# Half-array matmuls for the sorted keys, and for the values of batch 1, in a fused Sinkhorn-attention and feed-forward kernel

## The chip, the cores and the metric

The kernel runs on one core of a Trainium2 chip. The core has a matrix engine (TensorE, rows PE for the matmuls and PEld for the loads of their weights), a vector engine (VectorE, DVE), a scalar engine (ScalarE, ACT), a general engine (GpSimd, POOL) and a queue engine (SyncE, SP) that issues DMAs. Each takes its instructions in order. Two memories on the core matter here: SBUF, which holds operands, and PSUM, into which the matmuls write, from which VectorE and ScalarE read, and which has eight banks of 512 float32 in each of 128 partitions. The metric is device time in microseconds for one launch.

## The reference

Inputs are q, k and v of 4 batches x 8 heads x 768 tokens x 64, one 8x8 matrix `sort_net` for each head, and the weights of a feed-forward layer (512 to 2048 to 512).

```
P = sort_net; 5 times: P = exp(P - rowmax); P /= its row sums; P /= its column sums
k_sorted[i] = sum over j of P[i, j] * k_block[j]      # 8 blocks of 96 tokens, each head
v_sorted[i] = sum over j of P[i, j] * v_block[j]
attn = softmax(q_block @ k_sorted_block.T / 8)         # within a block of 96 tokens
x = (attn @ v_sorted_block), heads side by side        # 3072 x 512
out = (s * relu(x @ w_in)**2 + b) @ w_out
```

## The kernel before

All of k of a batch lies in one SBUF tile `RAW["k", b]`: 128 partitions are (head, block, z), where z says which half of a block's 96 tokens; the free axes are 48 tokens c and 64 values d. `build_pd` makes from P a matrix `PD[b]` of 128 x (e, z, g), 2 x 2 x 32 columns: head 2a+e, half z, and g = (a, i) for the pair of heads a and the sorted block i. It is zero except where row and column belong to the same head and half, so that a matmul with `PD[b]` as the moving operand sorts the blocks of all heads at once. Row half 0 to 63 holds heads 0 to 3, that is the pairs a = 0 and 1 and the columns g = 0 to 15; row half 64 to 127 holds the others.

**Keys.** `k_piece` and `k_banks` (batch 0) are not touched. `k_pairs` (batches 1 to 3) takes 16 tokens c. For each two of them it issues one matmul (L314): weights are 128 partitions x (2 tokens x 64 values), 128 columns of `PD` move, and the result is (token parity u, d) x (e, z, g). After 8 such matmuls, which fill two banks of the tile `tpp`, four copies move it into `KS`, 64 partitions x 512 elements each: the two of e = 0 by one engine and the two of e = 1 by the other (L203 is the copy on ScalarE, L205 the one on VectorE, both inside the helper `evac`). The letters "DA" or "AD" say which engine has which.

**Values.** `v_piece` (batches 0 and 1) needs values with d outside and tokens inside. For batch 1 `permute` makes this tile `VP[1]`: 2 x 16 columns d on ScalarE (L195), the other 32 on GpSimd in four copies (L197). Then one column d at a time is the weight (128 partitions x 64), and two matmuls, one for each z, write the two halves of the PSUM partitions (L340): 32 matmuls for 16 columns d. One copy of 112 x 1024 moves them to `VS`. Batches 2 and 3 sort values by another way (`v_tiles`, `v_back`), which stays.

**The order.** The schedule is written out by hand: every engine executes its instructions in the order in which the Python code issues them. For a batch b the two feed-forward halves run as `ffn1(2b)`, `ffn1(2b+1)`, `ffn2(2b)`, `ffn2(2b+1)`. `ffn2` (L525) is three row blocks m of 16 matmuls (128 x 512, `ops`); after every fourth there is a slot, 0 to 11, in which work of the next batch is issued. After the 16th of a block, and before the work of that slot, `store` (L550) has VectorE take `ops` out of PSUM. `halves(n)` returns the slots of batch n: K pieces `KP`, V pieces `V`, score pieces `SC` (matmul L405, exp on ScalarE L413), `P` (attention times values, L450, then a reciprocal L455 and a product L456 on VectorE), `TD` (a transposing DMA of the result, L476), and `PDB`, which is `build_pd` of the batch after, seven small VectorE instructions (L275 to L294).

**Buffers.** The PSUM pool `psa` has three buffers of two banks. K, V, score and P pieces and the tiles of `ffn1` take them in turn, so that each has to wait until the one three before it has been read out. The pool `psb` has two buffers of one bank; `ops` alternates between them.

**Queries.** For batches 1 to 3 q comes through two transposing DMAs per batch (`q_dma`, L484, tile `qt`) issued on SP behind the DMAs of `v_back` (L379, L383).

Of the kernel before, what the change touches and what calls it, by code (L numbers as in the profile page):

```python
# [9 lines left out]
FP = mybir.dt.float32  # L10
# [12 lines left out]
def kernel(  # L23
# [12 lines left out]
    nc = tc.nc  # L36

    B, H, S, D = q.shape
# [9 lines left out]
    C2 = BLK // 2  # L48
    GAP = 64
    KR = GAP + C2  # L50
    NG = NHP * NB
    VW = D + 2
    CK = 16
# [15 lines left out]
    psa = ctx.enter_context(tc.tile_pool(name="psa", bufs=3, space=bass.MemoryType.PSUM))  # L69
# [14 lines left out]
    RAW = {}  # L84
# [34 lines left out]
    VP = [const.tile([128, D, GAP], BF, name=f"vp{i}") for i in range(2)]  # L119
    KS = [const.tile([128, NG, 2, GAP], BF, name=f"ks{i}") for i in range(2)]  # L120
    VS = [const.tile([KR, 2 * NG, VW], BF, name=f"vs{i}") for i in range(2)]
# [67 lines left out]
    idv = ident.rearrange("p (a e j z) -> p a e j z", a=NHP, e=2, j=NB)  # L189

    def permute(eng, b, src, cs=slice(0, C2), ds=slice(0, D)):
        o = VP[b % 2][:, ds, cs]
        i = src[:, cs, ds].rearrange("p c d -> p d c")
        if eng is nc.scalar:
            eng.copy(out=o, in_=i)  # L195
        else:
            eng.tensor_copy(out=o, in_=i)  # L197
# [3 lines left out]
    def evac(eng, out, in_):  # L201
        if eng == "A":
            nc.scalar.copy(out=out, in_=in_)  # L203
        else:
            nc.vector.tensor_copy(out=out, in_=in_)  # L205

    def q_banks(b, half, engs):
# [3 lines left out]
        for u in range(2):  # L211
# [13 lines left out]
            out=jsel, in_=ident.rearrange("p (h j z) -> p j h z", h=H, j=NB), axis=AX.XY, op=ALU.add),  # L225
        lambda: nc.vector.tensor_reduce(
            out=bm.rearrange("p (e z a) -> p e z a", e=2, z=2),
# [26 lines left out]
    PD = {}  # L254
# [54 lines left out]

    def k_pairs(b, c0, engs):  # L310
        m = CK // 2
        ps = psa.tile([128, m, 2, 2 * NG], FP, tag="a", name="tpp")
        for j in range(m):
            nc.tensor.matmul(out=ps[:, j].rearrange("p e g -> p (e g)"),  # L314
                             lhsT=RAW["k", b][:, c0 + 2 * j:c0 + 2 * j + 2, :].rearrange(
                                 "p c d -> p (c d)"),
                             rhs=PD[b].rearrange("p e z g -> p (e z g)"), start=True, stop=True)
        for e in range(2):
            for u in range(2):
                evac(engs[e],  # L320
                     KS[b % 2][e * 64:(e + 1) * 64, :, :, c0 + u:c0 + CK:2],
                     ps[u * 64:(u + 1) * 64, :, e].rearrange("p c (z g) -> p g z c", z=2))

    def k_banks(b, c0, engs):
        for u, eng in enumerate(engs):
# [10 lines left out]
    def v_piece(b, d0, eng, halves=None):  # L336
        ps = psa.tile([128, CK, 2 * NG], FP, tag="a", name="tv")
        for d in range(CK):
            for z in range(2):
                nc.tensor.matmul(out=ps[z * GAP:(z + 1) * GAP, d, :],  # L340
                                 lhsT=VP[b % 2][:, d0 + d, :], rhs=PD[b][:, :, z, :],
                                 start=True, stop=True)
        if halves is None:
            evac(eng, VS[b % 2][:, :, d0:d0 + CK], ps[0:KR].rearrange("p d g -> p g d"))
            return None

        def half(h, eng):
            hs = slice(h * HB, (h + 1) * HB)
            evac(eng, VS[b % 2].rearrange("p (g i) w -> p g i w", i=NB)[:, :, hs, d0:d0 + CK],
                 ps[0:KR].rearrange("p d (g i) -> p g i d", i=NB)[:, :, hs])  # L350

        half(0, eng)
        return lambda eng: half(1, eng)

    NC = C2 // 8

# [34 lines left out]
    def s_piece(b, half, hp, sc=None):  # L391
        g0 = hp * NB + half * HB
        if sc is None:
            sc = psa.tile([128, 2, 512], FP, tag="a", name="sc")
        byp = len(QT[b].shape) == 5
        for n in range(HB):
            for e in range(2):
                pr = slice(e * 64, (e + 1) * 64)
                if byp:
                    o = sc[:, e, 0:TG].rearrange("p (c t) -> p c t", c=CQ)[:, :, 16 * n:16 * n + 16]  # L400
                    r = QT[b][pr, half, hp, :, 16 * n:16 * n + 16]
                else:
                    o = sc[:, e, n * BLK:(n + 1) * BLK]
                    r = QT[b][pr, half * HB + n, hp, :]
                nc.tensor.matmul(out=o, lhsT=KS[b % 2][pr, g0 + n].rearrange("p z c -> p (z c)"),  # L405
                                 rhs=r, start=True, stop=True)
        at = atp.tile([KR, 2, TG], BF, tag="at", name="at")
        if byp:
            nc.scalar.activation(out=at.rearrange("p e (t c) -> p e t c", c=CQ),
                                 in_=sc[0:KR, :, 0:TG].rearrange("p e (c t) -> p e t c", c=CQ),  # L410
                                 func=AF.Exp, scale=scale)
        else:
            nc.scalar.activation(out=at, in_=sc[0:KR, :, 0:TG], func=AF.Exp, scale=scale)  # L413
        AT[b, half, hp] = at
# [150 lines left out]
    s_piece(0, 0, 1, sc1)  # L565
    v_piece(0, CK, "D")
    v2 = v_piece(0, 2 * CK, "D", 1)
    v3 = v_piece(0, 3 * CK, "A", 1)
    v2("D")
# [18 lines left out]
    def v_sort(b, r=range(8)):  # L588
        for i in r:
            permute(nc.gpsimd, b, RAW["v", b], ds=slice(i * 8, (i + 1) * 8))  # L590
# [26 lines left out]
    def K(b, i, eng): return lambda: k_piece(b, i * CK, eng)  # L617
    def KP(b, i, engs="DA"): return lambda: k_pairs(b, i * CK, engs)
    def V(b, i, eng): return lambda: v_piece(b, i * CK, eng)
    def SC(b, h, i): return lambda: s_piece(b, h, i)  # L620
    def P(b, h, i): return lambda: p_piece(b, h, i)
    def TP(b, h, i, eng): return lambda: t_piece(b, h, i, eng)
# [2 lines left out]
    def TD(b, h): return lambda: t_dma(b, h)  # L625
    def PDB(b): return lambda: build_pd(b, later[:, b % 2, b // 2, :])
# [4 lines left out]
    def halves(n):  # L631

        if n == 1:
            s0 = {3: [KP(n, 0, "AD"), KP(n, 1, "AD"), KP(n, 2, "AD")],
                  9: [V(n, 0, "D"), V(n, 1, "A"), V(n, 2, "D")]}
        else:
            s0 = {0: [KP(n, 0), KP(n, 1), KP(n, 2)]}
        s1 = {0: [SC(n, 0, 0), SC(n, 0, 1)],
              3: [P(n, 0, 0), SC(n, 0, 2), SC(n, 0, 3)], 4: [P(n, 0, 1)], 5: [P(n, 0, 2)],
              6: [P(n, 0, 3), TD(n, 0), SC(n, 1, 0), SC(n, 1, 1)], 8: [P(n, 1, 0)],  # L640
              9: [P(n, 1, 1), SC(n, 1, 2), SC(n, 1, 3)], 10: [P(n, 1, 2)],
              11: [P(n, 1, 3), TD(n, 1)]}
        if n == 1:
            s1[0] = [V(n, 3, "A")] + s1[0]
        if n + 1 < B:
            s1[1] = [PDB(n + 1)]
        return s0, s1

    ffn1(0, {0: [QF0()], 2: [SB(0)], 3: [P(0, 1, 0), SB(1)], 4: [P(0, 1, 1), SB(2)],
# [10 lines left out]
    for d in (0, CK):  # L660
        permute(nc.scalar, 1, RAW["v", 1], ds=slice(d, d + CK))
    after(GT[1][:, NF - 1, 0:1])
    v_sort(1, range(4, 8))
    load("v", 2, 6, QT[1][:, NB - 1, 0, 0:1])
    s0, s1 = halves(1)
    ffn2(0, s0)
    ffn2(1, s1)
    for b in range(1, B):
        n = b + 1
        s0, s1, u0, u1 = {}, {}, {}, {}  # L670
        if n < B:
            load("k", n, 6, XT[2 * b + 1][:, HB - 1, NHP - 1, 0:1])
            load_q_rows(n)
            s0, s1 = halves(n)
# [37 lines left out]
```

## Time and profile before

| | |
|---|---|
| median of 3 runs | 221.51 us (221.34 to 221.83) |
| profiled execution | 221.32 us, its span 219.6 us |
| granted TensorE clock | 1.000 |
| PE / DVE / ACT / POOL busy | 97% / 56% / 50% / 32% of the span |
| keys of batches 1, 2, 3 on PE (L314) | from 53.57, 101.42 and 149.42 us, 24 matmuls each |
| values of batch 1 on PE (L340) | from 60.19 us (96 matmuls) and from 64.52 us (32) |

Times in the views are microseconds from the start of the span. A row of the timeline gives the start, the time from the first start to the last end of a group of like instructions, and in brackets the idle time of the engine ahead of it with what ended it. Matmuls are pipelined: the busy time of a group ends one matmul's own duration (about 0.2 us for the small ones) after the last start, while the next one may already have started. So the cost of a group on PE is read from its start to the start of the next group. A record may be missing here and there; runs of 11 or 23 `ops` stand where the code issues 12 or 24.

### The profile page before, as it was taken

The page shows a single profiled execution, that of the slowest core. Times are in us where ns is not written, and L with a number is a line of the kernel's source. Part 1 is how long each engine was busy: PE and PEld are TensorE (multiplying, and loading weights), DVE is VectorE, ACT ScalarE, POOL GpSimd, SP SyncE. Part 2 cuts the span into 40 slices and gives each one's busy share as a digit, 9 for nine tenths or more (in the row PEclk, how much of TensorE's full clock was granted, in tenths as well). Part 3 has the DMA queues.
Part 4 walks back from the last instruction along what each step waited for, and adds up shares of the span by engine and source line. Part 5 has one row for each costly group of instructions (what it writes and reads, how often), then busy time and mean ns, then how long its engine had stood idle before and what let it go on. Part 6 is the DMA issues. An engine that isn't in the chain of part 4 may idle for free.

```text
span 219.6 us, 5281 instructions
## 1 busy us (share of the span) xinstructions
PE 213.2 (97%) x2208; PEld 128.5 (59%) x2227; DVE 123.8 (56%) x256; ACT 110.8 (50%) x153; POOL 71.3 (32%) x127
## 2 busy tenths in 40 slices
PE   7999999999999999999999999999999999999994
PEld 5977766655465555556446555666445555654454
DVE  6777456566884767446636686448417744441222
ACT  4687687658626346664622546665425355650000
POOL 7659872689914003950006008720000000000000
DMA  6999999999979753999998955999991580001212
GB/s 155 281 166 124 122 170 207 204 171 139 128 199 136 105 159 62 184 188 117 98 176 198 210 119 74 211 165 95 87 237 51 119 122 0 0 0 51 95 49 96
DMA packets 68023, 28.92 MB, mean 132 GB/s; under 512 B 51872, under 2 KB 64288, under 8 KB 68000
## 3 DMA queue, kind: packets, MB, share of 16 engines
q0 software_dynamic: 31168, 12.85, 50.5%
q1 hardware_dynamic: 36832, 15.74, 39.7%
q8 instruction: 17, 0.28, 0.6%
q14 instruction: 6, 0.05, 0.1%
HBM read 28.85 MB, written 7.86 MB: 167 GB/s over the span
## 4 chain that ended last, share of the span: by engine, by line
PE 96%; DVE 2%; issue 1%; ACT 0%
PE hps L501 38%; PE ops L525 36%; PE z L130 5%; PE pv L450 4%; PE sc L405 3%; PE tpp L314 2%; PE ops L542 2%; PE tv L340 2%; DVE vs L205 1%; PE tr L467 1%; PE scb L423 1%; PE tp L304 1%; PE tvr L367 1%; PE sc L259 0%; PE pv L444 0%
## 5 line engine op out<-in xcount | busy, mean ns | idle before, releaser
L501 PE MATMUL hps<-xt,wi 128*128 128x384 bf16 x512 | 86.6, 326 | 0.0
L525 PE MATMUL ops<-wo,gt 128*128 128x512 bf16 x350 | 82.0, 379 | 1.4 <-issue 0.6
L513 ACT ACTIVATE rt<-hps 128x768 bf16<-128x768 f32 x64 | 51.8, 811 | 37.1 <-PE hps L501 36.4
L501 PEld LDWEIGHTS <-wi 128*128 128x128 bf16 x512 | 48.7, 98 | 32.1 <-issue 0.8
L514 DVE TENSOR_TENSOR gt<-rt 128x768 bf16<-128x768 bf16 x64 | 35.5, 557 | 42.5 <-ACT rt L513 42.4
L525 PEld LDWEIGHTS <-gt 128*128 128x128 bf16 x368 | 34.1, 98 | 37.4
L550 DVE SCALAR_TENSOR_TENSOR ot<-ops,s_bc,bias 128x512 f32<-128x512 f32 (+2 forms) x27 | 18.6, 691 | 34.9 <-PE ops L525 31.1
L413 ACT ACTIVATE at<-sc 112x768 bf16<-112x768 f32 x24 | 18.1, 808 | 30.0 <-PE sc L405 30.0
L456 DVE TENSOR_TENSOR x<-pv,rec 96x512 bf16<-96x512 f32 x32 | 22.0, 686 | 1.1
L115 POOL DMA_DIRECT2D qtok<-in_q_dram x24 | 18.6, 795 | 5.2 <-DMA rawk<-in_k_dram 3.1
L450 PEld LDWEIGHTS <-at 112*128 112x128 bf16 (+1 forms) x256 | 12.8, 101 | 6.7 <-ACT at L413 1.0
L203 ACT CAST ks<-tpp 64x512 bf16<-64x512 f32 x18 | 13.1, 727 | 4.7 <-DVE ks L205 4.1
L140 POOL DMA_DIRECT2D wi<-in_moe_w_in_dram x24 | 13.0, 563 | 4.8 <-DMA rawk<-in_k_dram 3.1
L450 PE MATMUL pv<-vs,at 112*128 112x66 bf16 (+1 forms) x256 | 13.7, 195 | 0.1
L205 DVE CAST ks<-tpp 64x512 bf16<-64x512 f32 x18 | 13.1, 729 | 0.8 <-ACT ks L203 0.5
L93 POOL DMA_DIRECT2D rawk<-in_k_dram x21 | 11.2, 549 | 3.1 <-issue 1.9
L130 PE MATMUL z<-zeros 128*64 128x96 bf16 (+2 forms) x129 | 10.6, 254 | 1.3 <-DVE zeros L118 1.2
L93 POOL DMA_DIRECT2D rawv<-in_v_dram x18 | 9.7, 556 | 5.5 <-DMA wo<-in_moe_w_out_dram 4.0
L90 POOL COPY rawk<-xt 128x1 bf16<-128x1 bf16 x2 | 1.0, 488 | 29.4 <-DMA xt<-x 29.4
L130 PEld LDWEIGHTS <-zeros 128*64 128x64 bf16 (+1 forms) x130 | 8.3, 126 | 3.0 <-DVE zeros L118 1.2
L455 DVE RECIPROCAL rec<-pv 96x8 f32<-96x8 f32 x32 | 6.4, 200 | 6.3 <-PE pv L450 6.3
L90 POOL COPY rawv<-qt 128x1 bf16<-128x1 bf16 x2 | 0.4, 190 | 22.0 <-DMA qt<-qtok 22.0
(98 smaller groups left out, 143.9 us busy)
## 6 DMA issues: line engine op xcount, KB each, us to landing
out_dram<-ot SPq DMA_DIRECT2D x22, 256.0 KB, 2.4
rawv<-in_v_dram POOLq DMA_DIRECT2D x18, 128.0 KB, 5.8
rawk<-in_k_dram POOLq DMA_DIRECT2D x18, 128.0 KB, 4.3
qtok<-in_q_dram POOLq DMA_DIRECT2D x24, 96.0 KB, 7.5
wo<-in_moe_w_out_dram POOLq DMA_DIRECT2D x4, 512.0 KB, 10.4
v0f<-in_v_dram SPq DMA_DIRECT2D x4, 384.0 KB, 5.8
vd<-rawv SPq DMA_DIRECT2D x8, 192.0 KB, 6.3
vs<-vd SPq DMA_DIRECT2D x4, 384.0 KB, 11.9
```

What stands on the lines that cost most here:

```text
L93: nc.gpsimd.dma_start(out=ti[:, c:c + n, :].rearrange("p c d -> p (c d)"), in_=raw["qkv".index(t)][b][:, c * D:(c + n) * D])
L115: nc.gpsimd.dma_start(out=QTOK[b][:, n], in_=qv[:, n])
L130: nc.tensor.matmul(out=z[0:m, 0:w], lhsT=zeros[:, 0:m], rhs=zeros[:, 0:w], start=True, stop=True)
L205: nc.vector.tensor_copy(out=out, in_=in_)
L413: nc.scalar.activation(out=at, in_=sc[0:KR, :, 0:TG], func=AF.Exp, scale=scale)
L450: nc.tensor.matmul(out=pv[0:m, e, n * VW:(n + 1) * VW], lhsT=atf[:, c0:c0 + m], rhs=VS[b % 2][:, e * NG + g(n), :], start=True, stop=True)
L456: nc.vector.tensor_tensor(out=x[:, :, hp * 128:(hp + 1) * 128].rearrange("p n (e d) -> p e n d", e=2), in0=pvv[:, :, :, 0:D], in1=rec.unsq ...
L501: nc.tensor.matmul(out=H1[t, i][:, f, 0:TG], lhsT=wi[:, hp, fc:fc + 128], rhs=XT[t][:, :, hp, :], start=(hp == 0), stop=(hp == NHP - 1))
L513: nc.scalar.activation(out=rt, in_=h, func=AF.Relu)
L514: nc.vector.tensor_tensor(out=gt[:, 2 * i:2 * i + 2, :], in0=rt, in1=rt, op=ALU.mult)
L525: nc.tensor.matmul(out=ops, lhsT=gt[:, f, m * 128:(m + 1) * 128], rhs=wo[:, f, :], start=(f == 0), stop=(f == NF - 1))
L550: nc.vector.scalar_tensor_tensor(out=ot[:, ns], in0=ops, scalar=s_bc, in1=BIAS[0][:, ns], op0=ALU.mult, op1=ALU.add)
```

## The change

`k_pairs` issues for each two tokens two matmuls instead of one: the weights are the upper or the lower 64 partitions, and only the 64 columns of `PD` move that belong to them. The upper half writes the first bank of the tile, the lower half the second. The four copies keep their sizes and their engines, but read across the two banks.

Batch 1's values get the new `v_pairs`: two columns d are the weights of one matmul (64 partitions x 128), again once for each row half, 16 matmuls for 16 columns. Four copies follow, of 64 x 512 (z = 0) and 48 x 512 (z = 1), the two of u = 0 by one engine, the two of u = 1 by the other; u is the half of the PSUM partitions. So that a copy writes eight neighbouring d, `permute` lays the columns of `VP[1]` out in another order. Piece 0 moves from slot 9 to slot 7 of the first `ffn2`, with all four copies on ScalarE; pieces 1 and 2 stay in slot 9 and piece 3 in slot 0 of the second `ffn2`, two copies on each engine. `PDB` of batch 2 moves from slot 1 to slot 7 of the second `ffn2`. `PDB` of batch 3 stays.

```diff
     def permute(eng, b, src, cs=slice(0, C2), ds=slice(0, D)):
-        o = VP[b % 2][:, ds, cs]
-        i = src[:, cs, ds].rearrange("p c d -> p d c")
+        if b == 0:
+            o = VP[0][:, ds, cs]
+            i = src[:, cs, ds].rearrange("p c d -> p d c")
+        else:
+            g = ds.start // CK
+            o = VP[1].rearrange("p (g j u) c -> p g u j c", j=CK // 2, u=2)[:, g, :, :, cs]
+            i = src[:, cs, g * CK:(g + 1) * CK].rearrange("p c (u j) -> p u j c", u=2)
+            if ds.stop - ds.start < CK:
+                u = ds.start % CK // (CK // 2)
+                o, i = o[:, u], i[:, u]
...
     def k_pairs(b, c0, engs):
         m = CK // 2
-        ps = psa.tile([128, m, 2, 2 * NG], FP, tag="a", name="tpp")
+        ng = NG // 2
+        ps = psa.tile([128, 2, m, 2, 2, ng], FP, tag="a", name="tpp")
         for j in range(m):
-            nc.tensor.matmul(out=ps[:, j].rearrange("p e g -> p (e g)"),
-                             lhsT=RAW["k", b][:, c0 + 2 * j:c0 + 2 * j + 2, :].rearrange(
-                                 "p c d -> p (c d)"),
-                             rhs=PD[b].rearrange("p e z g -> p (e z g)"), start=True, stop=True)
+            for r in range(2):
+                pr = slice(r * 64, (r + 1) * 64)
+                nc.tensor.matmul(out=ps[:, r, j].rearrange("p e z g -> p (e z) g"),
+                                 lhsT=RAW["k", b][pr, c0 + 2 * j:c0 + 2 * j + 2, :].rearrange(
+                                     "p c d -> p (c d)"),
+                                 rhs=PD[b].rearrange("p e z g -> p (e z) g")[
+                                     pr, :, r * ng:(r + 1) * ng],
+                                 start=True, stop=True)
         for e in range(2):
+            ks = KS[b % 2].rearrange("p (r g) z c -> p r g z c", r=2)[e * 64:(e + 1) * 64]
             for u in range(2):
-                evac(engs[e],
-                     KS[b % 2][e * 64:(e + 1) * 64, :, :, c0 + u:c0 + CK:2],
-                     ps[u * 64:(u + 1) * 64, :, e].rearrange("p c (z g) -> p g z c", z=2))
+                evac(engs[e], ks[:, :, :, :, c0 + u:c0 + CK:2],
+                     ps[u * 64:(u + 1) * 64, :, :, e].rearrange("p r c z g -> p r g z c"))
...
+    def v_pairs(b, d0, engs):
+        m = CK // 2
+        ng = NG // 2
+        ps = psa.tile([128, 2, m, 2, 2, ng], FP, tag="a", name="tvp")
+        for j in range(m):
+            for r in range(2):
+                pr = slice(r * 64, (r + 1) * 64)
+                nc.tensor.matmul(out=ps[:, r, j].rearrange("p e z g -> p (e z) g"),
+                                 lhsT=VP[b % 2][pr, d0 + 2 * j:d0 + 2 * j + 2, :].rearrange(
+                                     "p d c -> p (d c)"),
+                                 rhs=PD[b].rearrange("p e z g -> p (e z) g")[
+                                     pr, :, r * ng:(r + 1) * ng],
+                                 start=True, stop=True)
+        for u in range(2):
+            for z in range(2):
+                w = (GAP, C2)[z]
+                o = VS[b % 2][z * GAP:z * GAP + w, :, d0 + u * m:d0 + (u + 1) * m]
+                evac(engs[u], o.rearrange("p (e r g) d -> p e r g d", e=2, r=2),
+                     ps[u * 64:u * 64 + w, :, :, :, z].rearrange("p r d e g -> p e r g d"))
...
+    def VP2(b, i, engs): return lambda: v_pairs(b, i * CK, engs)
...
         if n == 1:
             s0 = {3: [KP(n, 0, "AD"), KP(n, 1, "AD"), KP(n, 2, "AD")],
-                  9: [V(n, 0, "D"), V(n, 1, "A"), V(n, 2, "D")]}
+                  7: [VP2(n, 0, "AA")], 9: [VP2(n, 1, "AD"), VP2(n, 2, "AD")]}
...
         if n == 1:
-            s1[0] = [V(n, 3, "A")] + s1[0]
+            s1[0] = [VP2(n, 3, "AD")] + s1[0]
         if n + 1 < B:
-            s1[1] = [PDB(n + 1)]
+            s1[7 if n == 1 else 1] = [PDB(n + 1)]
```

## The prediction

> **What bounds the kernel now.** I read the page's busy times and chain first, then the timeline of PE around the three groups that change, then VectorE, ScalarE and the query DMAs around them.
>
> ```profile
> PE 213.2 (97%) x2208; PEld 128.5 (59%) x2227; DVE 123.8 (56%) x256; ACT 110.8 (50%) x153; POOL 71.3 (32%) x127
> PE hps L501 38%; PE ops L525 36%; PE z L130 5%; PE pv L450 4%; PE sc L405 3%; PE tpp L314 2%; PE ops L542 2%; PE tv L340 2%; DVE vs L205 1%; PE tr L467 1%; PE scb L423 1%; PE tp L304 1%; PE tvr L367 1%; PE sc L259 0%; PE pv L444 0%
> ```
>
> PE is the chain from end to end, so time cut from PE counts unless something else then makes PE wait. The changed groups are `tpp` and `tv`. PE's timeline in batch 1:
>
> ```profile
> 53.57 1.50 PE L314 MATMUL tpp<-pd,rawk 128*128 128x128 bf16 x24
> 54.91 5.34 PE L525 MATMUL ops<-wo,gt 128*128 128x512 bf16 x23
> 60.19 1.71 PE L340 MATMUL tv<-pd,vp 128*64 128x64 bf16 x96
> 62.05 2.54 PE L525 MATMUL ops<-wo,gt 128*128 128x512 bf16 x11 [0.16 <-issue]
> 64.52 0.69 PE L340 MATMUL tv<-pd,vp 128*64 128x64 bf16 x32
> 65.15 0.51 PE L405 MATMUL sc<-qt,ks 64*128 64x96 bf16 x16
> 65.82 2.54 PE L525 MATMUL ops<-wo,gt 128*128 128x512 bf16 x11 [0.16 <-issue]
> ```
>
> Keys cost 54.91 - 53.57 = 1.34 us for 24, 56 ns each. An `ops` matmul costs 0.216 (three of them from 148.77 to the keys at 149.42). Runs of 11 lack their first record, so `ops` resumes at 61.84 and at 65.60. `tv` goes in pairs that fill the array side by side: (1.71 - 0.20)/47 = 32 ns a pair. `sc` has the shape that the change gives to keys and values, half the rows and 128 columns of weights, but 96 moving columns: (0.51 - 0.20)/7 steps, some 43 ns a pair. Batch 3 shows what it costs to go into such pairs and out again:
>
> ```profile
> 150.76 10.52 PE L525 MATMUL ops<-wo,gt 128*128 128x512 bf16 x47
> 161.21 0.51 PE L405 MATMUL sc<-qt,ks 64*128 64x96 bf16 x16
> 161.66 2.76 PE L525 MATMUL ops<-wo,gt 128*128 128x512 bf16 x11
> ```
>
> 48 x 0.216 from 150.76 ends at 161.12; `sc` starts 0.09 later. Its last pair starts at 161.52 and `ops` 0.14 after that. The full-array `tpp` pays neither. Copies, from ScalarE's timeline, VectorE's, and the list of those that work on `ks`:
>
> ```profile
> 54.22 4.45 ACT L203 CAST ks<-tpp 64x512 bf16<-64x512 f32 x6 [0.22 <-PE tpp L314]
> ```
> ```profile
> 55.72 4.50 DVE L205 CAST ks<-tpp 64x512 bf16<-64x512 f32 x6 [0.45 <-ACT ks L203]
> ```
> ```profile
> L205 DVE CAST ks<-tkb x1: 681/681/681, 15.4 to 15.4; 128x512 bf16<-128x512 f32 x1
> L203 ACT CAST ks<-tkb x1: 591/591/591, 15.7 to 15.7; 128x512 bf16<-128x512 f32 x1
> ```
>
> 512 elements take 0.73 on either engine where every second element is written (`tpp`), 0.59 and 0.68 where eight neighbours are (`tkb`). VectorE's half of a key piece starts only when ScalarE's is done. VectorE where `PDB` leaves and where it arrives:
>
> ```profile
> 64.44 0.22 DVE L275 TENSOR_TENSOR tmp<-later,jsel 128x64 f32<-128x64 f32 x1
> ...
> 65.80 0.25 DVE L294 SCALAR_TENSOR_TENSOR pw<-bmz,rc,pt 128x32 bf16<-128x32 f32 x1
> ```
> ```profile
> 74.04 0.75 DVE L550 SCALAR_TENSOR_TENSOR ot<-ops,s_bc,bias 128x512 f32<-128x512 f32 x1 [0.49 <-PE ops L525]
> 75.17 0.20 DVE L455 RECIPROCAL rec<-pv 96x8 f32<-96x8 f32 x1 [0.38 <-PE pv L450]
> 75.41 0.69 DVE L456 TENSOR_TENSOR x<-pv,rec 96x512 bf16<-96x512 f32 x1
> ```
>
> Last, the queries of batch 2 (the tile `qt` from 95 to 118 us):
>
> ```profile
> L484 SPq DMA_TRANSPOSE qt<-qtok x2: 1431/5094/8756, 102.4 to 111.3; - x2
> ...
> DMA to landing us min/median/max: 3.9/7.3/10.7
> ```
>
> The first lands at 102.4 + 10.7 = 113.1; the first `sc` of batch 2 starts at 113.23.
>
> **The change part by part.** A pair of row halves with 64 moving columns isn't in the trace. Bounds: 28 ns (`sc` scaled by 64/96) and 43 (`sc` as it is). I take 32, from `tv`, with as many moving columns.
>
> *Keys, per batch.* 1.34 becomes 0.09 + 23 x 0.032 + 0.14 = 0.97: 0.37 saved (0.13 at 43 ns, 0.46 at 28). The key copies keep size and engines; they read across two banks, as `tpp`'s do now. They end about 0.1 earlier with their matmuls.
>
> *Batch 2's share.* PE would reach the first `sc` 0.37 earlier, but its queries land when it starts now. The two DMAs are issued on SP behind `v_back`, whose first DMA at 86.3 follows copies that follow PE at 83; so the landing moves with what happened by then, not with the keys at 101. I book 0 (bounds: 0 and -0.37). In batch 3 `qt` lands at 160.1 and `sc` starts at 161.21: 0.37 goes through.
>
> *Values on PE.* Before, slot 9 costs 61.84 - 60.10 = 1.74, slot 0 with its `sc` 65.60 - 64.43 = 1.17. After: slot 7 0.09 + 7 x 0.032 + 0.14 = 0.45, slot 9 0.09 + 15 x 0.032 + 0.14 = 0.71, slot 0 0.09 + 8 x 0.032 + 7 x 0.043 + 0.14 = 0.79. Saved 0.96 (0.64 at 43 ns, 1.07 at 28).
>
> *Value copies.* Four copies of 1.0 to 1.2 us become sixteen; with eight neighbours written I take `tkb`'s 0.60 and 0.69 with the gaps (up to 0.73). ScalarE is done with the keys at 58.6, then: piece 0 to 61.0, piece 1 to 62.2, piece 2 to 63.4. VectorE ends its keys and the store at 60.9, then piece 1 to 62.3, piece 2 to 63.7, the store, piece 3 to 65.8. PE, 1.3 early by then, wants piece 2's buffer for the second score piece of slot 0 at about 64.0, and `VS` whole for the first `P` at 66.8. So they cost nothing, if the two engines copy one piece at the same time: ScalarE reads partitions 0 to 63, VectorE 64 to 127, where for the keys both read the same partitions. At 0.73 the second score piece waits 0.4. The other bound is the first rival.
>
> The Trainium skill, "PSUM — Partial Sum Buffer", section on bank collisions, says that two engines may use one bank at once in different groups of 32 partitions but not in the same group, reads included. The keys' wait agrees; no run here shows the other half. By it the copies of a value piece run side by side, and the sum is the one below.
>
> *`permute`.* Same elements (2 x 1.5 us on ScalarE, 4 x 0.83 on GpSimd), another order of writing. ScalarE's end at 54.0 and the key copies come at 54.1: a slower one delays them. GpSimd's last ends at 60.06 and is needed after 63: covered up to twice its length.
>
> *`PDB` in slot 7.* The seven instructions take 66.05 - 64.44 = 1.61. In slot 7 they follow the store, which ends at 74.79, and stand ahead of L455 and L456 of `P(1,1,0)`. Those now end at 76.09 and would end at 74.71 + 1.61 + 0.93 = 77.25. In the turn of three buffers (P, SC, SC | P | P, SC, SC) the last score piece of slot 9 takes the buffer which that L456 empties. It starts at 76.34 now (half of the `sc` group at 76.20), 0.25 after it is free. So PE stands for 1.16 - 0.25, with the hand-over 0.95 (0.85 to 1.05). Nothing behind hides it; the transposing DMA of slot 6 gains slack. What leaves slot 1 gives PE nothing: VectorE is idle there from 66.05 to 68.40.
>
> *Sum.* -0.37 - 0.96 + 0.95 + 0 - 0.37 = -0.75. Of the profiled execution's 221.32 (span 219.6) that makes 220.6; it lies 0.19 under the median of the runs, so on the median 220.8.
>
> **The rivals.**
>
> *Copies of one value piece one after the other* (slower). If what holds the second engine back in the keys is the tile's bank and not its partitions, VectorE starts piece 1 after ScalarE's 62.2, ends at 63.6, and piece 2 at 65.1. The second score piece of slot 0 waits from 64.0 to 65.1: +1.1, all on PE (2.0 at 0.73 per copy). For it: on the key tiles, the only ones that two engines copy, one waits for the other; against: there they share partitions. Sum +0.35: 221.9, up to 222.8. It decides from a wait of 0.75 on.
>
> *The pairs run no faster than `sc`'s.* Twice 0.24 less from the keys, 0.32 less from the values: +0.05, 221.6. For it, that no weight load of 128 columns with fewer moving columns runs in pairs; against, `tv`.
>
> *Weight loads of the two halves one after the other.* `pv` gives a load of 128 columns with its matmul every 33 ns; two are 65. Keys then cost 0.09 + 23 x 0.065 + 0.14 = 1.73, +0.39 in three batches, and the values save 0.96 - 30 x 0.033 = 0. With 0.95: +2.1, 223.6. Against it: two such loads fit into `sc`'s 43 ns. The Trainium skill, "TensorE: Matmul & The Clock Gate", section on LDWEIGHTS, has a load's time go by its columns and not by its rows, which speaks for this rival; the same 43 ns show that it isn't so one after the other.
>
> *`PDB` costs no wait*, because the buffers turn otherwise than I read: -1.70, 219.8.
>
> **How the numbers follow.** Forecast 0.41; copies in turn 0.32; pairs as slow as `sc` 0.09; loads in turn 0.04; no wait for `PDB` 0.08; some delay that I don't see, such as slower copies through two banks, 0.06 at about +0.8. The forecast's own range is 220.2 to 221.3; with the rivals 219.9 to 222.4, which leaves out about 0.15. 0.2% is 0.44 us, about what a measurement of this kernel tells from no change. Faster: 0.35 of the forecast and the 0.08 without a wait, 0.43. Within: 0.05 of the forecast, 0.11 of the copies in turn, 0.05 of the pairs as slow as `sc`, 0.21. Slower: the rest, 0.36.
>
> **What would show it.** Keys: 48 matmuls in about 0.97. Values: groups of 16, 32 and 16 at 32 ns a pair. Copies: VectorE's first `vs` copy of piece 1 starts while ScalarE's run, or when they end. `PDB`: PE stands inside the `sc` group of slot 9, about 0.95, released by L456. Batch 2: PE waits for `qt` at the first `sc`. Wrong would make it: a PE wait at slot 0, a pair well off 32 ns, or queries that come earlier.

## The result, and the profile after

The kernel after takes 222.77 us (median, 221.4 to 225.77), the one before 221.73 us in the same session: ratio 1.0047 [1.0031, 1.0063]. It is slower, by 1.04 us, where 0.75 us less was forecast, and it lies above the forecast range of 219.9 to 222.4. The profiled execution takes 221.90 us, with a span of 219.8. First the page after: busy times, and the chain that ended last by engine.

```profile
PE 211.0 (96%) x2216; PEld 125.4 (57%) x2235; DVE 125.5 (57%) x260; ACT 115.0 (52%) x161; POOL 71.1 (32%) x127
PE 88%; DMA 5%; DVE 3%; issue 1%; POOL 1%; ACT 1%; POOLq 0%
```

PE is busy for 2.2 us less than before (213.2), and its share of the span went from 97% to 96%: the work is shorter, and waits fill the place. The timeline of PE in batch 1 shows the first wait (start, duration of the group, group; in brackets the idle time and its releaser):

```profile
54.05 0.87 PE L325 MATMUL tpp<-pd,rawk 64*128 64x64 bf16 x48
55.08 3.40 PE L558 MATMUL ops<-wo,gt 128*128 128x512 bf16 x15 [0.16 <-PE tpp L325]
58.42 0.41 PE L375 MATMUL tvp<-pd,vp 64*128 64x64 bf16 x16
58.76 1.90 PE L558 MATMUL ops<-wo,gt 128*128 128x512 bf16 x8
60.59 0.64 PE L375 MATMUL tvp<-pd,vp 64*128 64x64 bf16 x32
61.39 2.54 PE L558 MATMUL ops<-wo,gt 128*128 128x512 bf16 x11 [0.16 <-PE tvp L375]
63.86 0.41 PE L375 MATMUL tvp<-pd,vp 64*128 64x64 bf16 x16
64.10 0.33 PE L438 MATMUL sc<-qt,ks 64*128 64x96 bf16 x8
65.56 0.35 PE L438 MATMUL sc<-qt,ks 64*128 64x96 bf16 x8 [1.12 <-ACT vs L211]
```

The new groups are as short as forecast or shorter. Keys: (0.87 - 0.19)/23 = 30 ns a pair, and the weight loads of the two halves of a pair start 3 to 4 ns apart in the trace, as their matmuls do; with 0.09 of entry ahead of the group and 0.13 after its last start a batch of keys costs 0.91 in place of 1.34. Values cost 0.43, 0.67 and about 0.80 in slots 7, 9 and 0, together 1.90 in place of 2.91. But in slot 0 the `sc` group, 16 matmuls in one run before, is now cut in two: its second piece would start at 64.27 (four pairs of 43 ns after 64.10) and starts at 65.56, 1.29 later. What it waits for is in the timelines of ScalarE and VectorE around it, and in the durations of the tile `tvp` (min/median/max ns, first and last start):

```profile
58.95 4.79 ACT L211 CAST vs<-tvp 64x512 bf16<-64x512 f32 x8
64.31 1.18 ACT L211 CAST vs<-tvp 64x512 bf16<-64x512 f32 x2 [0.56 <-PE tvp L375]
```
```profile
60.49 0.75 DVE L583 SCALAR_TENSOR_TENSOR ot<-ops,s_bc,bias 128x512 f32<-128x512 f32 x1
62.58 2.83 DVE L213 CAST vs<-tvp 64x512 bf16<-64x512 f32 x4 [1.34 <-ACT vs L211]
```
```profile
L211 ACT CAST vs<-tvp x10: 582/585/591, 59.0 to 64.9; 64x512 bf16<-64x512 f32 x5, 48x512 bf16<-48x512 f32 x5
L213 DVE CAST vs<-tvp x6: 693/694/695, 62.6 to 66.9; 64x512 bf16<-64x512 f32 x3, 48x512 bf16<-48x512 f32 x3
```

VectorE is free at 61.24 and begins with its half of piece 1 at 62.58, when ScalarE's six copies of pieces 0 and 1 are done (58.95 + 6 x 0.60 = 62.55). The wait is written in the program: in the trace that first copy waits for a semaphore which ScalarE raises with its last copy of the piece, 62.55, beside the one of PE. Its four copies of pieces 1 and 2 end at 65.41, and then piece 2's buffer is free for the second score piece. The bracket of that `sc` names ScalarE, whose last copy of piece 3 ends at 65.49; piece 3 is in another buffer, and 0.15 us lie between VectorE's end and the `sc`.

Slot 9 of the second `ffn2` has the second wait. PE's timeline, then VectorE's:

```profile
76.44 0.34 PE L438 MATMUL sc<-qt,ks 64*128 64x96 bf16 x8
77.45 0.34 PE L438 MATMUL sc<-qt,ks 64*128 64x96 bf16 x8 [0.67 <-DVE x L489]
```
```profile
74.28 0.75 DVE L583 SCALAR_TENSOR_TENSOR ot<-ops,s_bc,bias 128x512 f32<-128x512 f32 x1 [0.49 <-PE ops L558]
74.95 0.22 DVE L283 TENSOR_TENSOR tmp<-later,jsel 128x64 f32<-128x64 f32 x1
...
76.31 0.25 DVE L302 SCALAR_TENSOR_TENSOR pw<-bmz,rc,pt 128x32 bf16<-128x32 f32 x1
76.48 0.20 DVE L488 RECIPROCAL rec<-pv 96x8 f32<-96x8 f32 x1
76.71 0.69 DVE L489 TENSOR_TENSOR x<-pv,rec 96x512 bf16<-96x512 f32 x1
```

The seven instructions of `PDB` stand ahead of the reciprocal and the product of `P(1,1,0)`, and the second score piece starts 0.05 after that product's end: 77.45 where 76.60 was due, 0.85 us.

Batch 2, PE and then the queries (the time from issue to landing is in the last line):

```profile
102.60 0.87 PE L325 MATMUL tpp<-pd,rawk 64*128 64x64 bf16 x48
103.64 10.31 PE L558 MATMUL ops<-wo,gt 128*128 128x512 bf16 x47 [0.16 <-issue]
113.88 0.51 PE L438 MATMUL sc<-qt,ks 64*128 64x96 bf16 x16
```
```profile
L517 SPq DMA_TRANSPOSE qt<-qtok x2: 1431/4544/7658, 103.5 to 111.3; - x2
...
DMA to landing us min/median/max: 3.8/6.6/9.3
```

In this execution the first queries land at 103.5 + 9.3 = 112.8, ahead of the `sc` at 113.88, and there is no wait.

To put lengths on the stages I cut the spans at ScalarE's first or last relu of a `ffn1` (the start of the instruction L546 in the trace). The table gives the start up to the last relu of `ffn1(1)`, the stretches in which batches 1, 2 and 3 are prepared, all from the profiled execution, and the part of the device time that lies outside the span, the median of the timed runs, which differ in it by up to 0.13 within a kernel (their spans are on record to 0.1). The stretches between are the same in all kernels (20.33, 20.34, 19.50 and a tail of 23.66). The last columns are the median of the timed runs and the ratio to the kernel before in its own session, whose medians were 221.37 to 221.73. The medians count every run, while the ratios and the part outside leave out the few in a slow state, so the two don't always go together (`whole_pieces`: median 221.44, ratio 0.9981).

| kernel | start | batch 1 | batch 2 | batch 3 | outside | median | ratio |
|---|---|---|---|---|---|---|---|
| before | 50.32 | 30.10 | 27.66 | 27.64 | 1.78 | 221.73 | 1 |
| after | 50.70 | 30.81 | 27.21 | 27.22 | 2.14 | 222.77 | 1.0047 [1.0031, 1.0063] |
| after_again | 50.70 | 30.80 | 28.66 | 27.22 | 2.14 | 222.25 | 1.0044 [1.0016, 1.0072] |
| keys_only | 50.31 | 29.68 | 27.21 | 27.53 | 1.78 | 220.74 | 0.9967 [0.9946, 0.9987] |
| whole_pieces | 50.54 | 29.51 | 27.54 | 27.22 | 2.01 | 221.44 | 0.9981 [0.9951, 1.0012] |
| pdb_early | 50.19 | 29.96 | 28.68 | 27.21 | 2.14 | 221.74 | 1.0012 [0.9987, 1.0037] |
| by_bank | 50.44 | 31.80 | 27.58 | 27.22 | 1.78 | 224.48 | 1.0122 [1.0089, 1.0156] |
| before_pdb7 | 50.61 | 30.95 | 27.64 | 27.64 | 1.77 | 222.23 | 1.0034 [1.002, 1.0048] |
| before_qfirst | 50.20 | 30.10 | 27.64 | 27.64 | 1.78 | 221.29 | 0.9996 [0.9982, 1.001] |
| after_qfirst | 50.61 | 30.80 | 27.31 | 27.22 | 2.14 | 222.04 | 1.0027 [1.0014, 1.004] |
| after_spare | 50.12 | 30.82 | 27.21 | 27.21 | 1.77 | 222.36 | 1.0034 [1.0008, 1.006] |
| best | 50.56 | 28.72 | 27.21 | 27.21 | 2.01 | 220.51 | 0.9953 [0.9933, 0.9973] |
| best_qfirst | 50.64 | 28.71 | 28.57 | 27.22 | 1.99 | 220.19 | 0.9936 [0.991, 0.9961] |
| best_qfirst_spare | 50.07 | 28.66 | 28.17 | 27.21 | 1.82 | 219.40 | 0.9896 [0.987, 0.9921] |

Batch 1 carries the loss: +0.71, which is -0.43 for its keys, -1.01 for its values, +1.29 and +0.85 for the two waits (+0.70). Batch 3 gains 0.42. Batch 2 gains 0.45 in this execution. Outside the span 0.36 is lost. The start differs by as much as 0.6 between kernels that are alike up to there, and it differs between executions too: the shortest of the kernel after has a span of 219.2, 0.5 under the profiled one, whose later stretches have no wait left to lose but the two of batch 1. So I read nothing from it.

### The profile page after: what moved, and what is told of

It reads as the page before. It is cut to its first block, busy times and chain, and to the rows that moved or that the text cites. A ratio compares the mean times of both kernels' runs of the same rounds, so it can differ in the third digit from the quotient of the medians.

```text
span 219.8 us, 5315 instructions
## 1 busy us (share of the span) xinstructions
PE 211.0 (96%) x2216; PEld 125.4 (57%) x2235; DVE 125.5 (57%) x260; ACT 115.0 (52%) x161; POOL 71.1 (32%) x127
## 4 chain that ended last, share of the span: by engine, by line
PE 88%; DMA 5%; DVE 3%; issue 1%; POOL 1%; ACT 1%; POOLq 0%
PE hps L534 38%; PE ops L558 35%; DMA rawk<-in_k_dram 5%; PE pv L483 3%; PE sc L438 3%; PE ops L575 2%; PE tpp L325 1%; DVE vs L213 1%; PE tr L500 1%; PE scb L456 1%; PE tvp L375 1%; ACT vs L211 1%; PE tv L353 1%; PE tvr L400 1%; DVE ot L583 1%
## 5 line engine op out<-in xcount | busy, mean ns | idle before, releaser
L546 ACT ACTIVATE rt<-hps 128x768 bf16<-128x768 f32 x64 | 51.8, 811 | 37.6 <-PE hps L534 36.9
L583 DVE SCALAR_TENSOR_TENSOR ot<-ops,s_bc,bias 128x512 f32<-128x512 f32 (+2 forms) x27 | 18.6, 691 | 33.0 <-PE ops L558 26.5
L438 PE MATMUL sc<-qt,ks 64*128 64x96 bf16 x200 | 6.9, 204 | 2.0 <-ACT vs L211 1.1
```

The costliest lines, as they stand in the source:

```text
L546: nc.scalar.activation(out=rt, in_=h, func=AF.Relu)
L583: nc.vector.scalar_tensor_tensor(out=ot[:, ns], in0=ops, scalar=s_bc, in1=BIAS[0][:, ns], op0=ALU.mult, op1=ALU.add)
```

## The experiments

**The change again**: the kernel unedited, in another session.

> The changed kernel once more, unedited, for a second profile and more times. Theory A (two new waits of PE in batch 1): PE stands about 1.25 us in the middle of the score group of slot 0 (until ScalarE and VectorE have copied value piece 2 one after the other) and about 0.97 us in the middle of the score group of slot 9 (until VectorE, behind the seven PDB instructions, has emptied the buffer); both are the same in every execution, and the time lies 0.0 to 0.4 us over the kernel before. Rival B (the queries of batch 2): the two waits are there, but most of the 1 us by which the changed kernel is slower comes from executions in which PE also waits at the first score group of batch 2 for the transposing DMA, so that this profile shows a wait there, some tenths to 2 us, that the first profile did not.

Ratio 1.0044 [1.0016, 1.0072], so the loss repeats. Its profiled execution differs from the first in batch 2 alone: 28.66 in place of 27.21. PE there, and the queries:

```profile
103.39 10.53 PE L558 MATMUL ops<-wo,gt 128*128 128x512 bf16 x48
115.22 0.52 PE L438 MATMUL sc<-qt,ks 64*128 64x96 bf16 x16 [1.29 <-DMA qt<-qtok]
```
```profile
L517 SPq DMA_TRANSPOSE qt<-qtok x2: 1425/5314/9204, 104.3 to 113.7; - x2
...
DMA to landing us min/median/max: 3.8/7.3/10.8
```

The queries land at 104.3 + 10.8 = 115.1 and PE, which could have gone on 1.36 earlier, waits for them. Same program, same chain of DMAs: counted from the first DMA of `v_back`, the queries of batch 2 land after 25.3 us in one execution and 27.7 in the other (26.8 in the profile before), and PE wants them after 26.5. So the 0.43 that the keys of batch 2 save arrives in one of the two profiled executions, and in the other a wait of 1.4 stands there.

**The keys alone**: the kernel before with the new `k_pairs`, `V`, the slots and `PDB` as they were. The code, shortened:

```diff
-            nc.tensor.matmul(out=ps[:, j], lhsT=RAW["k", b][:, 2 tokens], rhs=PD[b])
+            for r in range(2):
+                nc.tensor.matmul(out=ps[:, r, j], lhsT=RAW["k", b][half r, 2 tokens],
+                                 rhs=PD[b][half r, the 64 columns of half r])
```

> The kernel before with the new key pieces alone (values, their slots and PDB as before). Keys cost 0.91 us a batch in place of 1.34. Theory A: 0.43 us saved in each of three batches, no new wait, 1.3 us faster than the kernel before (0.994). Rival B: batch 1 and 3 give 0.43 each, batch 2 gives nothing, because PE then waits about 0.4 us for the queries: 0.85 us faster or less (0.996 to 0.998), and the wait is seen ahead of the first score group of batch 2.

220.74, ratio 0.9967 [0.9946, 0.9987]: 0.73 faster. In the profiled execution batch 1 takes 0.42 less and batch 2 0.45, with no wait for the queries; batch 3 gives only 0.11: a store of VectorE starts at 164.28, when an output DMA queued on SP behind the queries has landed (164.16), the `P` behind it comes 0.17 late, and the first `hps` after the batch another 0.1. The profile bears out the saving of theory A on PE; the 0.73 of the medians lies nearer to the 0.85 of rival B, and its interval (0.29 to 1.2 us) tells the two apart only in part. What makes the kernel after slower comes with the values, with `PDB`, or outside the span, or with waits that they bring on later: 1.5 us on the medians (0.78 lost by after_again in the same session, and 0.73 gained here).

**One engine for each value piece**: only the letters of two pieces.

```diff
-                  7: [VP2(n, 0, "AA")], 9: [VP2(n, 1, "AD"), VP2(n, 2, "AD")]}
+                  7: [VP2(n, 0, "AA")], 9: [VP2(n, 1, "DD"), VP2(n, 2, "AA")]}
```

> The changed kernel with value piece 1 copied by VectorE alone and piece 2 by ScalarE alone, piece 0 and 3 as they are. No piece on which the next buffers wait has two engines any more. Theory A: piece 1 is free at about 64.0 and piece 2 at 63.8, the 1.25 us wait in slot 0 goes, the wait in slot 9 stays: 1.2 us faster than the changed kernel, 0.2 to 1.2 faster than before (0.995 to 0.999). Rival B: PE is 1.2 us earlier at batch 2 and waits there for the queries by as much; the time stays within 0.4 us of the changed kernel's. Third theory (the copies themselves, not their order, hold the buffers): the wait in slot 0 stays near 1.2.

VectorE's timeline, ScalarE's, and PE's in slot 0:

```profile
61.01 2.79 DVE L213 CAST vs<-tvp 64x512 bf16<-64x512 f32 x4
```
```profile
58.80 4.78 ACT L211 CAST vs<-tvp 64x512 bf16<-64x512 f32 x8
```
```profile
63.69 0.41 PE L375 MATMUL tvp<-pd,vp 64*128 64x64 bf16 x16
63.94 0.50 PE L438 MATMUL sc<-qt,ks 64*128 64x96 bf16 x16
```

VectorE now starts right behind its store, 2.6 us before ScalarE ends. The two engines write the same tile `VS` and read two different tiles `tvp`, and neither waits: that copy now has PE's semaphore alone to wait for. The `sc` group of slot 0 is whole again, and batch 1 takes 29.51: 1.30 less than after, which is the wait of 1.29. The wait in slot 9 stays. Ratio 0.9981 [0.9951, 1.0012], which can't be told from the kernel before.

**Copies dealt by PSUM bank** instead of by partitions: on pieces 1 to 3 ScalarE reads the first bank (row half r = 0) and VectorE the second, eight copies of 256 elements. The code, shortened:

```diff
+        for r in range(2):                      # where the two letters differ
+            for u in range(2):
+                for z in range(2):
+                    evac(engs[r], o.rearrange("p (e r g) d -> p e r g d", e=2, r=2)[:, :, r],
+                         ps[u * 64:u * 64 + w, r, :, :, z].rearrange("p d e g -> p e g d"))
```

> The changed kernel with the copies of value pieces 1 to 3 dealt to the two engines by PSUM bank (heads 0 to 3 to ScalarE, 4 to 7 to VectorE, four copies of 64 or 48 x 256 each) in place of by partitions. If the engines are kept apart by the bank: VectorE starts piece 1 at about 61.3, while ScalarE is at it, and not when ScalarE is done at 62.6; 256 elements take some 0.38 and 0.44 us (by the 512-element rows less 256 elements at the rate between the 512- and the 1024-element rows), piece 2 is free at about 64.9 in place of 65.4, and the wait in slot 0 falls from 1.25 to about 0.6. If they are kept apart on the whole tile: VectorE still starts after ScalarE's last copy, the wait grows to 2 us or more.

VectorE's timeline, ScalarE's, then PE's in slot 0:

```profile
60.26 0.75 DVE L590 SCALAR_TENSOR_TENSOR ot<-ops,s_bc,bias 128x512 f32<-128x512 f32 x1
62.66 3.49 DVE L213 CAST vs<-tvp 64x256 bf16<-64x256 f32 x8 [1.65 <-ACT vs L211]
```
```profile
58.71 7.00 ACT L211 CAST vs<-tvp 64x512 bf16<-64x512 f32 x16
```
```profile
64.49 0.35 PE L445 MATMUL sc<-qt,ks 64*128 64x96 bf16 x8 [0.48 <-ACT vs L211]
66.30 0.35 PE L445 MATMUL sc<-qt,ks 64*128 64x96 bf16 x8 [1.46 <-DVE vs L213]
```

VectorE begins its bank at 62.66, when ScalarE's four copies of the other bank, the fifth to the eighth of its sixteen, are done (62.63), just as with the split by partitions. With 0.37 and 0.42 us a copy in place of 0.59/2 and 0.69/2 for as many elements the wait grows, to some 2.3 in the two halves of the group, as expected for the whole tile: batch 1 takes 31.80, 0.99 more than in the kernel after, ratio 1.0122 [1.0089, 1.0156]. The last `sc` starts 0.15 after VectorE's end (66.15), the distance that the kernel after shows too. So neither this split of the partitions nor the one of the banks frees the second engine: the two engines' copies of one tile stand one behind the other, while those of two tiles don't. That is what this program's waits show; whether the chip itself would run them at once was not tried, since it would need the waits taken out.

**`PDB` in slot 7 alone**, in the kernel before:

```diff
-            s1[1] = [PDB(n + 1)]
+            s1[7 if n == 1 else 1] = [PDB(n + 1)]
```

> The kernel before with one part of the change alone: PDB of batch 2 in slot 7 in place of slot 1. Theory A: PE stands 0.9 to 1.0 us inside the score group of slot 9, as in the changed kernel (its step in the sum: 0.95); nothing else moves, so the time is 0.95 us over the kernel before, 1.0043. Rival: the wait only takes the place of a later one, as the one for the queries of batch 2; then the time rises by under 0.3.

PE's timeline in slot 9:

```profile
76.49 0.34 PE L405 MATMUL sc<-qt,ks 64*128 64x96 bf16 x8
77.50 0.34 PE L405 MATMUL sc<-qt,ks 64*128 64x96 bf16 x8 [0.67 <-DVE x L456]
```

Batch 1 takes 30.95, 0.85 more, and the median 0.86 more: ratio 1.0034 [1.002, 1.0048]. The wait is the move's own, without any of the new matmuls.

**`PDB` of batch 2 early**, in the second `ffn1`, where nothing of `P` stands behind it:

```diff
-        if n + 1 < B:
-            s1[7 if n == 1 else 1] = [PDB(n + 1)]
+        if 1 < n < B - 1:
+            s1[1] = [PDB(n + 1)]
-    ffn1(1, {2: [PDB(1)], 4: [make_bias]}, {0: 3, 1: 3})
+    ffn1(1, {2: [PDB(1)], 3: [PDB(2)], 4: [make_bias]}, {0: 3, 1: 3})
```

> The changed kernel with PDB of batch 2 in slot 3 of the second ffn1, where VectorE is idle, in place of slot 7 of the second ffn2. Theory A: the wait of 0.97 us in slot 9 goes, the wait of 1.25 in slot 0 stays: 0.95 us faster than the changed kernel. Rival B: PE waits for the queries of batch 2 by as much more, the time stays within 0.4 us of the changed kernel's.

PE's timeline in slot 9:

```profile
75.92 0.51 PE L438 MATMUL sc<-qt,ks 64*128 64x96 bf16 x16
```

The wait is gone: batch 1 takes 29.96, 0.85 less than after; the wait in slot 0 stays, at 1.28. Its profiled execution loses the gain again in batch 2 (28.68): 0.41 at the first `sc` for the queries, and 1.03 at a `P` whose buffer VectorE empties late, because the store ahead of that waits for an output DMA which is queued on SP behind the query DMAs and lands at 117.69. Ratio 1.0012 [0.9987, 1.0037], so on the median the gain shows in part: 0.51 us under after_again.

**Queries ahead of the values' return** on SP: the two DMAs that read the values back (`vs<-vd`, the end of `v_back`) are issued after the first query DMA of the batch. The code, shortened:

```diff
+        VD[b] = vd            # v_back ends here, its two reads become v_in(b)
...
+            if n0 == 0 and b in VD:
+                v_in(b)       # in q_dma, behind the first transposing DMA
```

> The changed kernel with one change of order on SP for batches 2 and 3: the first transposing DMA of the queries is issued ahead of the two DMAs that read the sorted values back, not behind them. In the profiles so far the first queries of batch 2 land 25.3 to 27.7 us after the first DMA that writes the values out, and the first score group comes 26.9 us after it in the kernel before and 26.5 in the changed one. Theory A+B (two fixed waits in batch 1 of 1.25 and 0.97, and a wait for the queries in batch 2 that differs from execution to execution and has grown by the 0.43 that the keys save there): the queries land some 15 to 20 us after the first write, the wait in batch 2 goes in all executions, the times draw together near the lower end of the changed kernel's (221.4 to 222.2), 0.3 to 1 us under its median. Theory A alone: same time as the changed kernel, within 0.3 us. Against both: the value DMAs, now behind, land after 30 us and PE waits for them at the first P.

> The kernel before with the queries of batches 2 and 3 first on SP, as in the run of the changed kernel. In the profile of the kernel before they land just when the first score group of batch 2 starts. If executions of it too lose time there, but less than the changed kernel (its limit is 26.9 us after the first write, that of the changed one 26.5), the median falls by 0.1 to 0.4 us and the upper quartile comes down; if not, it stays within 0.1.

The tile `qt` of after_qfirst:

```profile
L523 SPq DMA_TRANSPOSE qt<-qtok x2: 1489/3888/6288, 101.0 to 106.3; - x2
...
DMA to landing us min/median/max: 4.1/7.2/10.4
```

The first query DMA is issued at 101.0 and lands at 105.0, the second is issued at 106.3, five microseconds earlier than after's 111.3. The first queries of batch 2 land 17.7 us behind the first DMA of `v_back` in place of 25.3 to 27.7, and in this execution PE doesn't wait for them at the first `sc`. The runs of after draw together, from 221.39 to 223.77 down to 221.34 to 222.54, and the loss shrinks to 1.0027 [1.0014, 1.004]. The kernel before stays where it was, 0.9996 [0.9982, 1.001]; in its profile the queries landed 26.8 us behind that DMA and were wanted after 26.9. This fits a wait that the kernel after pays and the kernel before hardly does. It isn't shown beyond that: the interval still overlaps those of after (1.0047 and 1.0044), and the kernel with the keys alone, which wants the queries after the same 26.5 us, spreads by no more than 1.6. What is left of the loss is 0.59 us; batch 1, 2 and 3 and the part outside give 0.70 - 0.35 - 0.42 + 0.36 = 0.29, just under the measured interval (0.31 to 0.89).

**Six spare instructions on VectorE.** The part outside the span is 1.78 for before, 2.14 for after, and the same in every execution of a kernel within 0.13. The kernels differ in the number of VectorE's instructions. With its semaphore instructions, which the page leaves out, the traces hold 305 of them where the part outside is 1.77 or 1.78, 310 where it is 1.99 to 2.01, 312 where it is 2.14, but 318 in by_bank with 1.78 again; the expectation gives two more for each. So to the kernel after were added six small writes that nothing reads (the code, shortened):

```diff
+    spare = const.tile([128, 8], BF)
+        if b == 2:
+            u1 = {j: [lambda j=j: nc.vector.memset(spare[:, j:j + 1], 0.0)] for j in range(6)}
```

> The changed kernel with six more VectorE instructions of some 60 ns each (a spare column set to zero, one after each of six squares of the second ffn1 of batch 2, where VectorE has idle time). What it tells: the time outside the span is 1.78 us in the kernel before, with the keys alone and with the copies by bank, 2.0 with whole pieces and 2.14 in the changed kernel, the same in every execution of a kernel; the programs have 307, 307, 320, 312 and 314 VectorE instructions in this order. If that length is what it goes by, 320 brings it back to about 1.78, with the span as in the changed kernel (219.3 to 221.6); the time falls by 0.35. If it is the kind of copies or something else, it stays 2.14.

With these 318 instructions the part outside is 1.77. The 0.36 is thus no work of the change, since it goes while all of the change's work stays. It moves with the number of VectorE's instructions, though not in one direction; why, no run here shows. The whole time doesn't show the gain beyond its uncertainty: 0.99 us over before in its session, ratio 1.0034 [1.0008, 1.006], where after has 1.0047 and 1.0044.

**Both waits taken away**, then with the queries first, then with eight spare instructions as well (318 in the trace). The code, shortened:

```diff
+                  9: [VP2(n, 1, "DD"), VP2(n, 2, "AA")]}                 # as in whole_pieces
+    ffn1(1, {2: [PDB(1)], 3: [PDB(2)], 4: [make_bias]}, {0: 3, 1: 3})    # as in pdb_early
+            if n0 == 0 and b in VD: v_in(b)                              # best_qfirst and its spare
```

> The changed kernel with both waits of batch 1 taken away as in the two runs before: value pieces 1 and 2 copied by one engine each, PDB of batch 2 in slot 3 of the second ffn1. Theory A: 2.2 us faster than the changed kernel, 219.8 to 220.5, 0.5% under the kernel before. Theory B: the queries of batch 2 then bound the time as before, part of the executions wait there; median 220 to 221.3, spread over 2 us.

> The one before with the queries first on SP. Theory A+B: no wait left in batch 1 or at the queries of batch 2; every execution keeps what PE saves, 0.43 + 0.98 + 0.43 + 0.43 = 2.3 us under the kernel before, 219.2, and a spread of under 1 us. Theory A alone: as the one before.

> The kernel with whole pieces, PDB early and the queries first, with eight such spare instructions (320 on VectorE, as above). If the length goes with the time outside the span: 1.78 in place of 1.99, median about 219.9, 0.7% under the kernel before. If not: 220.2 as without them. In the last profile of the one without, one execution waited 1.1 us at the first ffn1 of batch 2 for the transposed result; if that is common, the upper half of the times stays up to 222.

220.51, 220.19 and 219.40 us: ratios 0.9953 [0.9933, 0.9973], 0.9936 [0.991, 0.9961] and 0.9896 [0.987, 0.9921]. Batch 1 takes 28.7, 1.4 less than before: the 0.43 + 1.01 of PE with no wait behind them. The last one beats the kernel before by 1%, and by the ratios the kernel after by some 1.5%. The one with the queries first misses what was expected of it, 219.2 with a spread under 1 us. In its profile batch 2 is long all the same (28.57): the first `hps` comes 1.60 after the last `P` (125.14 to 126.74) where best has 0.25: PE waits for the transposed result `xt`. Its DMA is issued at 120.1 in both and lands after 6.6 us here and after 4.9 in best; why, no run shows. PE's row:

```profile
126.74 1.47 PE L542 MATMUL hps<-xt,wi 128*128 128x384 bf16 x8 [1.18 <-DMA xt<-x]
```

## Why the prediction was wrong

*Keys.* Right. 30 ns a pair where 32 was taken (28 to 43), 0.09 of entry and 0.13 of exit as read from `sc`; 0.43 saved a batch where 0.37 was booked. The rival of pairs as slow as `sc` falls, and so does that of loads one after the other, which made a pair 65 ns: the two loads of a pair start 3 to 4 ns apart. In the rows of this case the step goes by the moving columns: 56 ns for 128 (`tpp` before), 43 for a pair with 96 (`sc`), 30 for a pair with 64. By the Trainium skill, "TensorE: Matmul & The Clock Gate", section on LDWEIGHTS, a load's time goes by its columns; that would have spoken for this rival only if the loads of two row halves went in turn, and the 3 to 4 ns between their starts show that they don't.

*Values on PE.* Right: 1.01 saved, 0.96 booked.

*Value copies.* This is the step that failed: "So they cost nothing, if the two engines copy one piece at the same time". The durations were right (0.585 and 0.694 for 0.60 and 0.69); the condition was not. ScalarE read partitions 0 to 63 and VectorE 64 to 127, and still VectorE began when ScalarE ended. The rival had the course: VectorE from 62.2 on, done at 65.1, a wait of 1.1; measured 62.58, 65.41 and 1.29. The threshold that it named, a wait of 0.75, was passed. The reason given there, "the tile's bank and not its partitions", is not right either: by_bank splits by banks and waits as well, and whole_pieces, with a tile for each engine, doesn't. The Trainium skill, "PSUM — Partial Sum Buffer", section on bank collisions, lets two engines read different groups of partitions at once. The traces here can neither show nor refute it, because the semaphores of the program put the second engine's copies behind the first engine's before such a collision could arise. Nor do the key copies agree with that section, as the prediction had it, or differ from it: VectorE's first copies of a key piece, too, wait in the trace of the kernel before for a semaphore of ScalarE (55.69, and VectorE starts at 55.72). I had put that down to their common partitions, and it was the warning.

*`PDB` in slot 7.* Right: 0.85 in the kernel after and 0.85 when moved alone (0.95 booked, 0.85 to 1.05). The rival that it costs no wait falls.

*Batch 2's keys.* Booked at 0 with -0.37 as the other bound. The right term has no fixed size: -0.45 in one profiled execution of the kernel after, +1.0 in the other, since the landing of the queries differs by 2.4 us from one to the other and the `sc` now stands inside that spread. The upper bound was missing: a DMA that is just in time for PE is late in some executions once PE comes earlier, and then the loss can be greater than the gain. pdb_early shows that it passes on to the store and to `P`.

*Batch 3.* Right: -0.42 for -0.37.

*Unforeseen.* 0.36 outside the span, which no line of the sum had.

The sum for the profiled execution was 220.6. Put right, with its own rows (the start's 0.38 is a difference that I can't put down to the change): 220.6 + 1.29 (slot 0) - 0.10 (`PDB`) - 0.45 (batch 2) - 0.12 (keys of batches 1 and 3) - 0.05 (values) + 0.36 (outside) + 0.38 (the start) = 221.9, as measured. On the medians, batches 1 and 3 and the part outside give 0.71 - 0.42 + 0.36 = 0.65 of the 1.04 in the first session and of the 0.78 in the second. The remaining 0.1 to 0.4 fit batch 2's waits, of which one of the two profiled executions has one; but no run puts a size on how often they come, and a start that is longer by 0.38 in most executions would fill the gap as well. That stays open. So does the question whether the waits come more often with the new values than with the new keys alone, whose runs stay between 220.32 and 221.94.

## What to carry to other kernels

When two engines are to empty one PSUM tile, look whether the trace has a tile that two engines read side by side; if in every one the second waits for the first, deal whole tiles to the engines, not parts of one (here 1.3 us). A group of small instructions moved on an engine that is only 57% busy can cost PE nearly all of its length as soon as it stands ahead of the instruction that empties PE's next buffer (here 0.85 of 1.61 us: VectorE had some idle time ahead of it, and PE had come to that buffer a little after it was free); look for a place with none of these behind it. A transfer that lands just in time bounds the saving of everything ahead of it, and by its spread over executions, not by the one execution in the profile.

## What the runs showed of the hardware beyond that

Time outside the span goes by the program and not by the run: 1.77 to 1.78 us with 305 instructions of VectorE in the trace, 1.99 to 2.01 with 310, 2.14 with 312, 1.77 to 1.82 with 318, and six instructions that do nothing took 0.37 back. For a change worth half a microsecond that is a term of its own, and its cause stays open. The landing of the transposing DMA of the queries differed by 2.4 us between two executions of one program, and moving two other transfers behind the first of them brought that landing 7.6 to 10 us forward and left the runs of the kernel within 1.2 us of each other where they had spread over 2.4 (after_again).
